# An H3 convolution and mixer kernel on one core: small loads as rows, angle arithmetic on ScalarE, and a re-dealt order of issue

## The chip, the core and the metric

The kernel runs on one core of a Trainium2 chip. A core has TensorE (PE, matrix products into PSUM), VectorE (DVE), ScalarE (ACT), GpSimd (POOL) and SyncE (SP, which here only starts DMA transfers). The metric is the device time of one execution in microseconds (us); lower is better.

## The reference

One sequence of S = 2048 tokens with D = 640 channels passes through two blocks, each with a conditioned LayerNorm in front and a gated residual behind:

```python
mod = (silu(c) @ w_mod).reshape(c.shape[0], 6, 1, -1)          # sa, ca, ga, sb, cb, gb
h = layernorm(x) * (1 + ca) + sa
x = x + ga * A_ref(h, k, v, shift_k, ssm_k, ssm_D)
h = layernorm(x) * (1 + cb) + sb
x = x + gb * B_ref(h, ...)

# A_ref
k_shift = sum(k_pad[:, t:t + S, :] * shift_k[:, ks - 1 - t] for t in range(4))
kv = k_shift * v
y = irfft(rfft(kv, 2 * S) * rfft(ssm_k, 2 * S))[:S] + kv * ssm_D
return q * y                                                     # q is the normed h

# B_ref
h = gelu(layernorm(x) @ w1)          # then four channel groups shifted by 1, -1, 2, -2 tokens
x1 = x + shifted(h) @ w2
return x1 + gelu(layernorm(x1) @ w3) @ w4
```

Here A_ssm_D and c are vectors of 640 values, and A_shift_k is a table of 640 x 4 values. D is folded into the long filter: it is added to the filter's first tap.

## The kernel before

Channels lie on the 128 partitions, in ND = 5 blocks of 128. The long convolution is a Fourier transform of length 4096 in two factors (64 x 64), done by matrix products. The stages are:

1. The filter A_ssm_k is loaded (tile Ra, five transfers at L228), D is added to its first tap (L444), each block is transposed on DVE into Rb (`to_slots`, L394), and `stage1` multiplies it with the small Fourier matrix F1bd (L407). Each result of 1024 columns is copied out of PSUM by ACT (L207) or DVE (L209) into T01.
2. `k_shift` (L463) applies the four-tap shift filter as products with diagonal matrices (tile RQ, built from skT by a POOL select at L355); DVE multiplies by v (L468). The products kv go through the same two stages.
3. `stage2_half` (L427) multiplies T01 with the second Fourier table Gs (in RG) into R3 for the filter and R5 for kv. Its groups go by k0, three of 32 at a time, in an order of their own.
4. `inverse1` multiplies both spectra on DVE (L617) and goes back by products with EA and EB (L628, L629); `inverse2` (L661) ends the transform.
5. `mod_half` (L493) makes the six modulation vectors from silu(c).
6. Then come the token tiles: LayerNorm chains (`chain_a`, `chain_b`, `chain_c`, `ln_finish`; L737 to L756, L702 to L717, sums of squares at L729), w1 (L818, L828), w2 (L873, L880), w3 (L907, L911), w4 (L928, L937), and the output.

The Fourier tables are computed in the kernel. `angles` makes integer angles: POOL counts (iota, L287), DVE multiplies and adds (L292), and masks (L293); ACT takes the sine (`sin_to`, L321). `angles_pool` does the same in floating point with a multiply-add (L306), a rounding (L308) and a subtraction (L310) on POOL or DVE; the sine is L316. F1bd is F1c put on a block diagonal by two POOL selects (L332, L333). Gs gets a first batch (kb = 0) by `angles` and a second (kb = 1) by `angles_pool`; a negated copy (L348) completes a batch. Then two transfers copy its upper half out (L353), and one copies the lower half into partitions 64 to 127 (L354), which must wait for the other two.

Every piece of work is a task with a number. The planner's `run` does not choose: the string ORDER lists all tasks in the order of issue, each with its engine (P, A, D, G for POOL, S for SP) and, for a task that takes PSUM, the places 0 to 3 of the four PSUM buffers. Each engine works through its tasks strictly in that order, and so does each DMA queue. Of the start, ORDER has on SP: D, blocks 1, 3, 2, 0 of A_ssm_k, the shift filter, block 4, and then the transposing loads of k and v (L233).

The three small operands are loaded with one element (or four) to a partition:

```python
dma("SP", 8, lambda q: ld_tiny(q, Dcol[:], A_ssm_D.rearrange("(b p) -> p b", p=P)), ...)
dma("SP", 8, lambda q: q.dma_start(skT[:], A_shift_k.rearrange("(b p) j -> p b j", p=P)), ...)
dma("SP", 8, lambda q: ld_tiny(q, c_col[:], c.rearrange("o (b p) -> p (o b)", p=P)), ...)
```

Of the kernel before, what the change touches and what calls it, by code (L numbers as in the profile page):

```python
# [8 lines left out]
BF = mybir.dt.bfloat16  # L9
F32 = mybir.dt.float32  # L10
I32 = mybir.dt.int32
ACT = mybir.ActivationFunctionType
# [14 lines left out]
0S 2S 19G 18D 50G 20D 21G 23D 22D 25A 4S 3S 1S 6S 27G 29D 36G 37G 28D 5S 8S 9S 11S 68G 10S 69D 24A 26G 88P:0 72G 73D 31A 30A 32D 38G 66D 89A 84P:1 85A  # L27
67D 90P:2 91A 86P:3 87D 39G 40A 102P:0 103A 100P:1 76P:2 70G 104P:0 41D 49G 101A 77A 42G 43G 105A 106P:3 107A 44A 45G 33S 47S 46S 71D 34S 12S 35S 48S
184S 181S 183S 182S 13S 14S 116P:1 92P:2 98P:0 74D 75D 117D 7S 99A 118P:3 119D 114P:0 15S 112P:1 113D 93A 110P:2 16S 115A 111A 96P:3 97A 94P:0 95D
82P:2 83A 80P:1 81A 78P:3 108P:0 51D 109A 52D 54A 56G 57D 53A 122P:2 79D 155P:1 156A 153P:0 154A 151P:3 152A 123D 157P:2 136D 120P:1 121D 173P:0 158A  # L30
55G 174A 171P:3 172A 177P:2 178D 175P:1 176A 161P:0 162D 141P:3 142A 167P:2 168D 147P:1 148A 58G 59G 163P:0 164D 165P:3 166A 137P:2 138A 145P:1 146A
230D 17S 149P:0 150A 190D 188D 126P:3 127D 139P:2 140A 60A 143P:1 199S 144A 124P:0 125D 179P:2 180A 187D 169P:3 170A 234P:1 235A 244P:2 159P:0 160A
128P:3 231D 242P:1 243A 245A 130P:0 61G 62G 186D 63G 64A 238P:1 239A 129D 131D 232D 248P:2 65G 196S 249A 246P:3 247A 185D 189G 191A 252P:0 202S 253A
134P:1 135D 132P:2 133D 236P:3 240P:1 237A 260P:0 261A 233D 250P:2 251A 241D 423D 200P:3 201A 258P:0 259D 319G 208S 192G 268P:2 269A 318S 197P:3 205S
198A 266P:1 267A 272P:2 273D 270P:3 271A 203P:0 284P:1 285A 292P:2 211S 204D 278P:3 279A 417D 276P:0 277A 342S 293D 426D 209P:1 210D 294P:2 295D 226S
290P:3 222G 291A 280P:1 281D 229G 227S 264P:0 274P:2 275D 343G 223G 265A 256P:3 262P:1 420D 206P:0 207D 257A 225G 254P:2 255D 282P:3 263A 286P:0
288P:1 287D 224G 312P:2 220S 283A 289A 212P:3 321D 320D 218G 213D 313A 328D 304P:0 305A 308P:1 316P:2 317A 217S 216G 302P:0 219S 214G 418D 228S 298P:2
215S 324P:3 325D 309A 221G 327G 326S 329D 322P:1 303A 336D 306P:0 299A 421D 323A 310P:2 296P:3 307A 334S 335G 337D 350S 297A 311A 300P:1 330P:0 301A
351G 332P:3 344D 345D 331A 314P:2 333A 315A 359G 340P:1 341A 338P:0 352D 348P:3 349A 353D 346P:2 358S 347A 360D 361D 354P:1 367G 339A 356P:3 368D 366S
369D 355A 364P:2 357A 375G 362P:0 376D 372P:1 374S 377D 401S 193A 363A 382S 370P:3 373A 384D 383G 385D 380P:0 378P:1 365A 392D 390S 391G 393D 422D  # L40
419D 424D 402P:2 427D 194D 403D 371A 388P:3 381A 379A 407S 389A 428D 386P:0 387A 416G 425D 396P:1 397A 394P:3 395A 398S 399P:0 400D 432P:12 429A 430D
434D 433A 489D 502A 510D 195G 413S 490D 491A 511D 530D 408P:3 513D 404S 405P:0 406A 531D 409A 512A 440S 492G 494D 475P:12 476A 477A 515D 532A 462P:03
463A 410S 411P:1 493G 495D 514G 435S 533D 534G 496A 497D 498G 441G 535D 464A 516D 536D 518D 499D 412A 517A 469P:20 537A 471A 519G 500P:3 538D 539G
414P:1 465G 470A 558D 449S 501D 520D 521P:3 436S 415A 507P:0 522A 443S 559D 560A 540D 541P:2 437S 542A 466P:13 431D 561D 562D 563A 564D 508A 546P:2
467D 468A 547A 548P:1 565G 448S 570D 528P:0 571D 566D 572D 567D 549A 573A 446S 568D 505P:3 506A 569A 574G 575G 447S 509G 529A 503D 523D 504D 621D 622D
472P:21 473A 526P:3 527A 623A 579D 580P:0 581A 576D 439S 543A 524D 577P:2 525D 624D 578D 625D 444S 438S 550P:3 627D 480S 551D 481S 626A 590P:0 591A
445S 482S 552A 588P:2 589A 595P:3 459D 628G 633D 629D 634D 553G 630D 631D 632A 635D 637D 636A 479S 554G 555D 556P:0 557A 592P:2 486S 596D 597A 638G
641A 639D 478S 488G 610P:3 612P:0 611A 593D 608P:2 606P:3 544D 594A 598D 613A 599G 474D 460A 603D 600D 601P:1 604P:0 609A 457D 607A 442S 454A 602A
640S 642S 651P:2 649P:3 461G 650A 450D 487S 652A 485S 605D 673P:0 667P:1 451D 545D 668A 674A 452G 582D 583D 484S 689D 690D 456A 458G 584D 585D 656P:3
692D 693D 653P:2 483S 614P:1 654D 655A 657D 694A 615D 659G 658A 671P:0 695D 660G 664D 665P:2 691A 661D 662P:3 663D 453D 669P:1 696G 701A 702D 703D  # L50
666A 735P:3 455G 672A 670A 697D 698D 699D 705G 737P:2 736A 739P:0 733P:1 616D 704A 643D 644D 645D 700A 738A 706G 709A 675P:32 710S 586D 587D 740A 755D
756D 757A 646A 707D 708S 758D 759D 717P:0 714D 761G 760A 762G 734A 763A 767D 777A 768D 711A 769D 719P:1 764D 780D 676P 718A 720A 721P:0 724P:1 647D
712D 765D 766A 677D 678D 770A 680S 771G 772G 683D 741P:32 648D 773D 774S 722D 775A 776S 785P:0 725D 726A 783P:1 713D 723A 824D 617S 825D 742P 821D
822D 827D 679S 681S 826A 743D 682S 727G 728G 731D 732S 823A 784A 828G 829A 786A 787P:3 729D 730S 833D 834D 835D 830D 831D 832A 837D 684D 685S 836A
620S 838G 790P:1 788D 789A 839D 840S 799P:0 791D 805P:3 806A 781D 841D 715D 716D 881D 749D 793G 792A 882D 842S 883A 803P:1 804A 794G 795A 796S 845P:2
846A 797D 778D 779D 884D 843P:3 844A 885D 887D 800A 801P:1 802A 618S 847P:2 848D 782D 941D 850P:3 851D 852A 886A 849A 619S 687S 798S 865P:0 866A
859P:1 860A 863P:2 807P:30 861P:1 744D 750D 753S 942D 944D 745S 853D 854G 855A 888G 893A 943A 752S 857A 889D 864A 945G 890D 856S 808P 858S 809D 891D
946A 947D 948D 950D 894D 862A 892A 895D 896A 897G 925P:2 926A 898G 751S 815D 747S 919P:3 901D 686S 920A 923P:1 899D 921P:0 949A 951G 922A 902S 900S
905P:2 906A 688S 903P:3 904A 952D 953S 956P:0 957A 954P:2 955A 907P:3 908D 910P:0 810D 958G 748S 959P:2 911D 913G 746S 816D 819S 924A 962P:1 867P:30
960D 817S 963D 813S 754S 912A 993P:2 909A 914G 812S 868P 915D 916S 917D 918S 977P:1 978A 994D 995A 996G 997G 971P:2 820S 972A 869D 998A 875D 927P:30  # L60
818S 964A 814S 811S 876D 961A 965D 966G 973P:1 967A 999S 969A 970S 870D 929D 974A 1028P:2 930D 975P:3 928P 968S 1000P:1 1001A 931S 935D 1002P:0 934S
976A 979P:13 981D 1003A 1006P:0 871S 873S 1004P:1 879S 1005A 872S 874S 936D 980P 987D 1029A 937S 933S 1026P:1 939S 1007A 877S 932S 988D 1024P:2 1025A
1032D 880S 878S 982D 983S 1008P:30 986S 991S 1027A 989S 1033D 1010D 938S 940S 1022P:2 1011D 1023A 1014S 1013S 1009P 1016D 984S 985S 1017D 1030P:13
1034D 992S 990S 1015S 1012S 1018S 1019S 1020S 1035D 1037S 1036S 1021S 1038S 1031P 1040D 1039S 1041D 1043A 1045A 1042S 1044S
# [72 lines left out]
def kernel(  # L137
# [51 lines left out]
    diagw = RQ[:, 0:2560].rearrange("p (b j m) -> p b j m", b=ND, j=4)  # L189
# [29 lines left out]
    c_col = mem.tile([P, ND], BF, name="c_col")  # L219
    skT = mem.tile([P, ND, 4], BF, name="skT")  # L220

    def ld_tiny(q, dst, src):
        with nc.allow_non_contiguous_dma(reason="tiny"):
            q.dma_start(dst, src)

    dma("SP", 8, lambda q: ld_tiny(q, Dcol[:], A_ssm_D.rearrange("(b p) -> p b", p=P)), w=[("Dcol", 0, 1)], rate=8.0)
    for b in range(ND):
        dma("SP", 512, lambda q, b=b: q.dma_start(sT[:, b, :], A_ssm_k[b * P:(b + 1) * P, :]), w=[("Ra", 2048 * b, 2048 * b + 2048)], rate=390.0)  # L228
    dma("SP", 8, lambda q: q.dma_start(skT[:], A_shift_k.rearrange("(b p) j -> p b j", p=P)), w=[("skT", 0, 1)], rate=30.0)
    dma("SP", 8, lambda q: ld_tiny(q, c_col[:], c.rearrange("o (b p) -> p (o b)", p=P)), w=[("ccol", 0, 1)], rate=12.0)  # L230
# [9 lines left out]
    b_neg = mem.tile([P, 1], F32, name="b_neg")  # L240
    stat = mem.tile([P, 3, 2, NT], F32, name="stat")
    s32 = mem.tile([P, 1], F32, name="s32")
    s32o = mem.tile([P, 1], F32, name="s32o")
    s64 = mem.tile([P, 1], F32, name="s64")
    s64t = mem.tile([P, 1], F32, name="s64t")
    pci = mem.tile([P, 2], I32, name="pci")
    offi = mem.tile([P, 2], F32, name="offi")
    offc = mem.tile([P, 6], F32, name="offc")

    def f(e):  # L250
        nc.vector.memset(mhalf[:], -0.5)
        nc.vector.memset(b_pos[:], PI_LO)
        nc.vector.memset(b_neg[:], -PI_LO)
        nc.vector.memset(stat[:], 0.0)
        nc.vector.memset(kT[:, :, 0:16], 0.0)
# [823 lines left out]
```

## Time and profile before

| | |
|---|---|
| Time, median of three runs (lowest, highest) | 301.91 us (301.49, 303.3) |
| Span of the profiled execution, first to last instruction | 298.7 us |
| Own time of the profiled execution beside its span | not given by the profile; 3.2 us lie between the span and the median |
| Busy: PE, DVE, ACT, POOL | 269.7, 218.2, 208.3, 104.8 us |
| Mean granted TensorE clock | 0.975 of full |
| DMA | 35.76 MB, 120 GB/s on average |
| Chain that ended last, by engine | PE 51%, DVE 13%, ACT 11%, DMA 10%, POOL 6%, issue 5% |

A profile comes from one execution on the chip. "L407" is line 407 of the kernel's file. A row names the engine, the operation, the tile written and the tile read with their shapes, a count, and a duration; "idle before <-X" is the time that the engine stood still just ahead, and what ended it. In the timeline the first column is the start in us from the span's start, the second the length. Neighbouring instructions of a kind are merged there ("x36"). A matmul's end is modelled, so a PE that is busy in every slice may still be paced by whoever empties its PSUM buffers.

### The profile page before, as it was taken

The page shows a single profiled execution, that of the slowest core. Times are in us where ns is not written, and L with a number is a line of the kernel's source. Part 1 is how long each engine was busy: PE and PEld are TensorE (multiplying, and loading weights), DVE is VectorE, ACT ScalarE, POOL GpSimd, SP SyncE. Part 2 cuts the span into 40 slices and gives each one's busy share as a digit, 9 for nine tenths or more (in the row PEclk, how much of TensorE's full clock was granted, in tenths as well). Part 3 has the DMA queues.
Part 4 walks back from the last instruction along what each step waited for, and adds up shares of the span by engine and source line. Part 5 has one row for each costly group of instructions (what it writes and reads, how often), then busy time and mean ns, then how long its engine had stood idle before and what let it go on. Part 6 is the DMA issues. An engine that isn't in the chain of part 4 may idle for free.

```text
span 298.7 us, 7890 instructions
## 1 busy us (share of the span) xinstructions
PE 269.7 (90%) x3176; PEld 208.5 (70%) x3182; DVE 218.2 (73%) x438; ACT 208.3 (70%) x341; POOL 104.8 (35%) x237
## 2 busy tenths in 40 slices
PE   0999999999989766869999999999999999999993
PEld 0666755777878436648878677787788767887871
DVE  8998999999999998898759589886361544212442
ACT  4799989999999789979868775766854705431200
POOL 5864364453216591434275426120421321100000
PEclk9999999999999859799999999999999999999999
DMA  6999999898999920563700203223113030510112
GB/s 215 275 215 184 225 137 246 225 217 221 229 253 281 280 65 2 153 203 69 273 4 0 46 5 68 56 46 60 41 40 80 5 89 6 63 43 23 29 52 60
DMA packets 58356, 35.76 MB, mean 120 GB/s; under 512 B 40032, under 2 KB 55008, under 8 KB 58320
## 3 DMA queue, kind: packets, MB, share of 16 engines
q1 hardware_dynamic: 57136, 32.01, 46.3%
q0 software_dynamic: 1088, 3.21, 4.1%
q8 instruction: 25, 0.41, 0.6%
q14 instruction: 11, 0.09, 0.1%
q10 hardware_dynamic: 96, 0.04, 0.1%
HBM read 16.31 MB, written 2.62 MB: 63 GB/s over the span
## 4 chain that ended last, share of the span: by engine, by line
PE 51%; DVE 13%; ACT 11%; DMA 10%; POOL 6%; issue 5%; SPq 2%; DVEq 0%; POOLq 0%; ACTq 0%
PE ps_w L937 17%; PE ps_w L907 14%; ACT T L207 5%; DMA Ra<-in_A_q_dram 5%; PE ps_w L873 4%; PE ps_w L818 3%; PE ps_s L427 3%; ACT RG L729 3%; DVE Rb L617 3%; PE ps_ksh L463 2%; POOL lnv L715 2%; PE ps_s L407 2%; DMA RK<-R 2%; DVE R L756 2%; PE ps_mod L493 2%
## 5 line engine op out<-in xcount | busy, mean ns | idle before, releaser
L907 PE MATMUL ps_w<-R,T 128*128 128x256 bf16 (+1 forms) x630 | 63.8, 261 | 0.7 <-DMA R<-RH 0.7
L907 PEld LDWEIGHTS <-T 128*128 128x128 bf16 x630 | 55.5, 98 | 7.9 <-issue 2.0
L937 PE MATMUL ps_w<-T,R 128*128 128x320 bf16 x416 | 59.1, 299 | 0.0
L911 ACT ACTIVATE R<-ps_w 128x1024 bf16<-128x1024 f32 (+2 forms) x36 | 28.8, 827 | 41.9 <-PE ps_w L907 41.9
L937 PEld LDWEIGHTS <-R 128*128 128x128 bf16 x416 | 40.5, 98 | 15.2
L960 DVE TENSOR_TENSOR T<-ps_w,R 128x640 bf16<-128x640 f32 x15 | 12.3, 822 | 35.4 <-PE ps_w L928 18.1
L207 ACT CAST T<-ps_s 128x1024 bf16<-128x1024 f32 x32 | 30.4, 1029 | 3.2 <-PE ps_s L407 3.1
L207 ACT CAST R<-ps_s 128x960 bf16<-128x960 f32 (+1 forms) x35 | 30.8, 964 | 1.8 <-PE ps_s L427 1.6
L407 PE MATMUL ps_s<-F1bd,Rb 128*128 128x256 bf16 x160 | 23.3, 298 | 8.7 <-DVE Rb L394 8.1
L729 ACT ACTIVATE RG<-R 128x640 bf16<-128x640 bf16 x32 | 23.5, 734 | 9.9 <-DVE R L880 6.7
L407 PEld LDWEIGHTS <-Rb 128*128 128x128 bf16 x160 | 16.7, 107 | 14.7 <-DVE Rb L394 8.6
L873 PE MATMUL ps_w<-RG,R 128*128 128x320 bf16 x160 | 23.2, 299 | 2.1 <-ACT R L820 2.1
L715 POOL TENSOR_TENSOR lnv<-lnv,mhalf 128x2 f32<-128x2 f32 (+1 forms) x29 | 22.5, 775 | 2.3
L427 PE MATMUL ps_s<-T,RG 64*128 64x160 bf16 x512 | 21.2, 230 | 0.8 <-ACT R L207 0.6
L880 DVE SCALAR_TENSOR_TENSOR R<-ps_w,R 128x640 bf16<-128x640 f32 x16 | 12.9, 819 | 11.8 <-PE ps_w L873 11.6
L427 PEld LDWEIGHTS <-RG 64*128 64x128 bf16 x512 | 17.7, 94 | 5.1 <-issue 4.6
L818 PE MATMUL ps_w<-R,RG 128*128 128x256 bf16 (+1 forms) x200 | 20.0, 259 | 1.3 <-DMA R<-RK 0.6
L873 PEld LDWEIGHTS <-R 128*128 128x128 bf16 x160 | 15.4, 98 | 8.2 <-ACT R L820 2.4
L629 PE MATMUL ps_i<-EB,Rb 128*128 128x128 bf16 x160 | 19.0, 219 | 1.5 <-DVE Rb L617 1.4
L818 PEld LDWEIGHTS <-RG 128*128 128x128 bf16 x200 | 17.1, 102 | 3.5 <-issue 2.0
L628 PE MATMUL ps_i<-EA,Rb 128*128 128x128 bf16 x160 | 19.0, 219 | 0.4 <-ACT R L207 0.3
L714 POOL TENSOR_TENSOR lnv<-stat,lnv 128x2 f32<-128x2 f32 x19 | 4.0, 212 | 40.9 <-ACT RG L729 28.7
(178 smaller groups left out, 513.5 us busy)
## 6 DMA issues: line engine op xcount, KB each, us to landing
Ra<-in_A_ssm_k_dram SPq DMA_DIRECT2D x5, 512.0 KB, 5.7
R<-in_w_mod_dram SPq DMA_DIRECT2D x6, 400.0 KB, 6.0
out_dram<-RH SPq DMA_DIRECT2D x60, 40.0 KB, 1.6
T<-in_B_w_dram SPq DMA_DIRECT2D x5, 432.0 KB, 6.2
RH<-in_w_mod_dram SPq DMA_DIRECT2D x4, 400.0 KB, 4.4
Ra<-in_A_q_dram SPq DMA_DIRECT2D x4, 320.0 KB, 6.6
RK<-R SPq DMA_DIRECT2D x5, 256.0 KB, 4.5
RK<-R POOLq DMA_DIRECT2D x5, 256.0 KB, 5.3
```

Source lines behind the costliest of these rows:

```text
L207: nc.scalar.copy(dst, src(ps.tile))
L407: nc.tensor.matmul(psv[:, ml, :], lhsT=xL[:, s0:s0 + P], rhs=F1r, start=True, stop=True)
L427: nc.tensor.matmul(psv[:, g, j], lhsT=Gs[p, k, 64 - 64 * cc:192 - 64 * cc], rhs=T1h[h][p, cc * 32 + k], start=(cc == 0), stop=(cc == 1), t ...
L628: nc.tensor.matmul(psv[:, w, :], lhsT=Av[:, r_, :, g_], rhs=EAf, start=True, stop=False)
L629: nc.tensor.matmul(psv[:, w, :], lhsT=Bv[:, r_, :, g_], rhs=EBf, start=False, stop=True)
L715: nc.gpsimd.tensor_tensor(rs, rs, mhalf[:, 0:n], ALU.pow)
L729: add("ACT", 0.74, lambda e: nc.scalar.activation(junk, src, ACT.Square, scale=float(D) ** -0.5, accum_out=stat[:, li, 1, t:t + 1]), r=[sk ...
L818: nc.tensor.matmul(pt[:, fb, 0:cw], lhsT=w1_sb[:, b, 160 * fb:160 * fb + P], rhs=hT[:, b, 0:cw], start=(b == 0), stop=(b == ND - 1))
L873: nc.tensor.matmul(pt[:, hf, 0:320], lhsT=gsf[:, fb, c0:c0 + P], rhs=w2_sb[:, fb, 320 * hf:320 * hf + 320], start=(fb == 0), stop=(fb == 4))
L907: nc.tensor.matmul(pt[:, fl, 0:cw], lhsT=w3_sb[:, b, fb * P:(fb + 1) * P], rhs=xT[:, b, 0:cw], start=(b == 0), stop=(b == ND - 1))
L911: nc.scalar.activation(g3[g % 2][:, f0:f0 + fn, 0:cw], ps.tile[:, 0:fn, 0:cw], ACT.Gelu_apprx_tanh)
L937: nc.tensor.matmul(bank(i, hf), lhsT=gg[:, fb, i * P:(i + 1) * P], rhs=w4_sb[:, fb, 320 * hf:320 * hf + 320], start=(fb == 0 and i == 0), ...
```

## The change

It has three parts.

**Rows.** D, c and the shift filter are loaded as five rows each (128, 128 and 512 elements) into a corner of T01 that is free at the start. TensorE turns them: a product with a 5 x 5 identity (`eye`, a POOL select) puts a row of 128 on 128 partitions. D takes one product and an ACT copy into Dcol; c and the four taps take five products and one ACT copy into `csk`, of which c_col and skT are now views. The diagonal matrices in RQ lie tap by tap instead of block by block.

**Angles.** The constant columns (`scol`) are split: nine operations stay on DVE, six go to a new POOL task (`scolt`). For the first batch of Gs, the multiply-add of `angles` leaves DVE for ACT (Identity with a scale and a bias column); DVE keeps the mask. The negated copy may now run on ACT too.

**Order.** The eight new tasks are put in, and some sixty tasks are moved in ORDER or given another engine. PSUM places change for 149 tasks.

```diff
@@ -216,18 +217,15 @@
-    dma("SP", 8, lambda q: ld_tiny(q, Dcol[:], A_ssm_D.rearrange("(b p) -> p b", p=P)), w=[("Dcol", 0, 1)], rate=8.0)
+    csk = mem.tile([P, 5 * ND], BF, name="csk")
+    c_col, skT = csk[:, 0:ND], csk[:, ND:5 * ND].rearrange("p (j b) -> p b j", j=4)
+    rowD, rowc, rows = T01[0:ND, 0:P], T01[0:ND, P:2 * P], T01[0:ND, 2 * P:6 * P]
+
+    dma("SP", 8, lambda q: q.dma_start(rowD, A_ssm_D.rearrange("(b p) -> b p", p=P)), w=[("T01", 0, P)])
...
-    dma("SP", 8, lambda q: q.dma_start(skT[:], A_shift_k.rearrange("(b p) j -> p b j", p=P)), w=[("skT", 0, 1)], rate=30.0)
-    dma("SP", 8, lambda q: ld_tiny(q, c_col[:], c.rearrange("o (b p) -> p (o b)", p=P)), w=[("ccol", 0, 1)], rate=12.0)
+    dma("SP", 8, lambda q: q.dma_start(rows, A_shift_k.rearrange("(b p) j -> b (p j)", p=P)), w=[("T01", 2 * P, 6 * P)])
+    dma("SP", 8, lambda q: q.dma_start(rowc, c.rearrange("o (b p) -> (o b) p", p=P)), w=[("T01", P, 2 * P)])
@@ -251,37 +250,62 @@
-    add("DVE", 1.9, f, r=[("pidx", 0, 1)], w=[("scol", 0, 1)])
+    add("DVE", 1.3, f, r=[("pidx", 0, 1)], w=[("scol", 0, 1)])
+
+    def f(e):
+        nc.gpsimd.tensor_scalar(s64t[:], s64[:], 1.0 / 8192, None, ALU.mult)
...
+    add("POOL", 1.0, f, r=[("scol", 0, 1)], w=[("scolt", 0, 1)])
+
+    add("POOL", 0.2, lambda e: nc.gpsimd.affine_select(out=eye, in_=one.to_broadcast([P, ND]), pattern=[[-1, ND]],
+                                                       compare_op=ALU.is_equal, fill=0.0, base=0, channel_multiplier=1),
+        r=[("consts", 0, 1), ("T01", 6 * P + 16, 6 * P + 17)], w=[("T01", 6 * P, 6 * P + ND)])
...
+        nc.tensor.matmul(pt[:, 0, 0:ND], lhsT=rowD, rhs=eye[0:ND, :], start=True, stop=True)
...
+    t1 = add("ACT", 0.2, lambda e: nc.scalar.copy(Dcol[:], psD.tile[:, 0, 0:ND]), w=[("Dcol", 0, 1)], use=psD)
...
+        nc.tensor.matmul(pt[:, 0, 0:ND], lhsT=rowc, rhs=eye[0:ND, :], start=True, stop=True)
+        for j in range(4):
+            nc.tensor.matmul(pt[:, 0, ND + ND * j:2 * ND + ND * j], lhsT=rows.rearrange("b (p j) -> b j p", j=4)[:, j, :], rhs=eye[0:ND, :], start=True, stop=True)
...
+    t1 = add("ACT", 0.2, lambda e: nc.scalar.copy(csk[:], psC.tile[:, 0, 0:5 * ND]), w=[("ccol", 0, 1), ("skT", 0, 1)], use=psC)
@@ -289,8 +313,12 @@
-                nc.vector.tensor_scalar(m_, ti, s_col, off, ALU.mult, ALU.add)
+                if not split:
+                    nc.vector.tensor_scalar(m_, ti, s_col, off, ALU.mult, ALU.add)
                 nc.vector.tensor_single_scalar(m_, m_, q - 1, ALU.bitwise_and)
+            if split:
+                add("ACT", 0.25 + 0.00095 * n, lambda e, m_=m_, off=off: nc.scalar.activation(m_, ti, ACT.Identity, scale=s_col, bias=off),
+                    r=[keys[0], ("scol", 0, 1)], w=[k_])
```

ORDER in the changed kernel, where it bears on what follows:

| Where | Before | After |
|---|---|---|
| SP, first issues | D, filter blocks 1, 3, 2, 0, shift filter, block 4; c much later (38.8 us) | block 3, D, block 1, shift filter, c, blocks 2, 0, 4 |
| ACT, first tasks | sines of F1c, sines of Gs | two multiply-adds of the angles, copy of Dcol, sines of F1c, sines of Gs, negation (first batch), copy of csk |
| PE, first tasks | stage 1 | product for Dcol, products for csk, stage 1 |
| Additions of D (L444) | blocks 1, 3, 2 POOL; 0, 4 DVE | blocks 3, 2, 4 POOL; 1, 0 DVE |
| Negation of Gs: first, second batch | DVE, POOL | ACT, DVE |
| Second batch, second angle: multiply-add, rounding, subtraction | DVE, POOL, POOL | POOL, DVE, DVE |
| H table, first multiply-add (L306 on RK) | DVE | POOL |
| Copies of Gs: three of batch 0, two of batch 1 | SP | POOL's queue |
| Stage-1 evictions, one each way | DVE and ACT | exchanged |
| LayerNorm statistics of two tiles (L539) | DVE | ACT |
| Norms: five, and two the other way | DVE, ACT | ACT, DVE |
| One transpose copy | ACT | DVE |
| First step of `ln_finish`, two groups | POOL | DVE |
| Two multiplies of q (L601) near 115 and 124 us, one w1 gelu | after the waits there | ahead of them; the gelu later |

Everything else keeps its engine, and nearly everything its neighbours. The output's transfers near the end are in a slightly different order.

## The prediction

> **What bounds the kernel now.** I read the page's rows by slice first, then windows of four microseconds, then the timeline of the first 26 us engine by engine, then the chain that ended last. The windows come first here (columns: window, length, busy us and instruction count of PE, weight loads, DVE, ACT, POOL, then clock, DMA share, GB/s).
>
> ```profile
> 8.00:10.00 2.00, 1.88 (x9) 1.35 (x10) 2.00 (x3) 0.81 (x1) 1.92 (x2) 1.00 1.02 328
> ...
> 20.00:24.00 4.00, 3.75 (x33) 2.98 (x32) 3.93 (x8) 4.00 (x6) 0.00 (x0) 1.00 0.89 189
> ...
> 116.00:120.00 4.00, 1.96 (x29) 1.64 (x27) 3.25 (x8) 3.90 (x10) 0.85 (x2) 0.98 0.00 0
> ...
> 128.00:132.00 4.00, 1.92 (x18) 1.45 (x17) 3.93 (x11) 3.69 (x9) 2.60 (x7) 1.00 0.86 287
> ...
> 180.00:200.00 20.00, 20.00 (x167) 15.86 (x166) 16.70 (x43) 12.37 (x27) 7.82 (x18) 1.00 0.30 63
> ```
>
> Three regimes follow. Until about 8 us nothing is multiplied. From 9 to 116 us DVE and ACT, which empty PSUM, are full, and PE follows them. From 116 to 140 PE is half idle while LayerNorm chains hop DVE, ACT, POOL. From 140 us PE has no gap worth speaking of, so the end is the moment it becomes full plus fixed work. A change counts only by how much earlier that moment comes.
>
> The start, in which most of the edit lies:
>
> ```profile
> 0.79 1.28 ACT L321 ACT_TABLE_LOAD   x1 [0.79 <-PEq L1063]
> ...
> 6.01 3.96 DVE L394 STREAM_TRANSPOSE Rb<-Ra 128x1024 int32<-128x1024 int32 x2
> ...
> 8.12 6.95 PE L407 MATMUL ps_s<-F1bd,Rb 128*128 128x256 bf16 x36 [8.12 <-DVE Rb L394]
> ...
> 9.19 2.84 ACT L207 CAST T<-ps_s 128x1024 bf16<-128x1024 f32 x3 [1.89 <-PE ps_s L407]
> ...
> 17.80 0.63 ACT L316 ACTIVATE RG<-R 128x512 bf16<-128x512 f32 x1 [0.52 <-POOL R L310]
> ```
>
> The first product waits for the first transpose, that for block 1 of A_ssm_k (landed 5.40) and its D add. Behind its table load ACT idles 2.06 us (to 4.13, for F1c's angles), 1.30 and 1.89 before its first eviction at 9.19; after that its only pause is 0.52 us at L316.
>
> The change, part by part.
>
> **Start.** (1) On DVE the scol step shrinks from 16 instructions (1.08 to 3.06) to 9; at the same spacing it ends near 2.4. Six go to POOL; its 128x1 rows are 189 to 354 ns, so 1.7 us, hidden, as POOL then waits for F1c. (2) ACT takes two 128x512 multiply-adds. The near row is L321 on 128x512, mean 715 ns, 1.34 us for two; on DVE they were 2 x 0.54. They stand first on ACT, and the built order of the changed kernel has a table load ahead of them, held until scol is done, and a second load ahead of the first Sin; before, one load ran at 0.79 for nothing. So: load 2.4 to 3.7, two Identity to 5.05, copy of Dcol to 5.35 (0.3, the 128x32 row), load to 6.65, two F1c sines to 7.2. Before, these ended at 4.66. (3) F1bd's two selects on POOL (2 x 0.42 and a gap) end at 8.15 instead of 6.84; the first product starts at 8.2 instead of 8.12. Slack eats nearly all 2.5 us. (4) ACT then has the RG sines (1.34), the negation (0.65, unseen on ACT; as its other 128x512 rows) and the copy of csk (0.25): free at 9.4, where 9.19 stood. (5) The add for block 3 stands behind F1bd on POOL, 8.35; DVE wants it at 7.95 and loses 0.4.
>
> Here two rules of the Trainium skill bear, both in "ScalarE: Activation LUTs". "What ACT_TABLE_LOAD costs" puts a switch at 2.66 us with its drain; the row of this kernel's other load, L834, is 1.28 (115.56 to 116.84, next ACTIVATE at 116.85), so I add 1.28; by the rule the first product would start 1.4 to 2.8 us later. "Rules for kernel authors" gives multiplies and adds to VectorE. Rows agree per piece (0.54 against 0.7), but ACT was idle here, so I book the load, not the pieces. That the load is needless (the page's "Table sets: the hidden batching unit" has identity in every set, and L547's Identity at 50.27 runs on the Sin set with no load between) changes nothing: the built order has it.
>
> **Rows and loads.** Dcol's load of single elements landed in 3.0 us, skT's in 6.6, c_col's in 5.0. As rows of 256 and 1024 bytes they are not in the trace: at least the 1.5 us of a 20 KB store, at most as before. SP now issues block 3 first, then D, block 1, rows, c. By bytes moved (770 KB by 5.40, some 400 KB/us after 4) a second half megabyte ahead costs block 1 about 0.7 us and the vanished element packets give about that back: 5.4 to 5.6, and at worst, with nothing given back, 5.40 + 0.51/0.4 = 6.7. D lands between 4 and 5, under the Identities. Six little products (a 98 ns weight load each) and two copies lie in idle PE and counted ACT time. The products of csk wait for c and the filter rows in front of the first stage-1 product, so rows landing after 8.2 would hold PE; expected 5.9. SP spends one more issue (0.58) ahead of the transposes, and none later.
>
> **POOL and DVE to 26 us.** POOL, 1.3 late, does L308 (1.97), a DMA issue (0.5), L310 (1.28), one add, the diagonal select (2.46): RQ ready near 15.0, not 13.07; PE wants it at 14.91, so 0.2 late. The second L308 and L310 and a negation leave POOL (4.7 us) for DVE (about 0.4 + 0.55 + 0.74; the TENSOR_SCALAR rows on DVE are 0.43 to 0.57), DVE gives away two L306 (1.1), one negation (0.74); evictions swap evenly. DVE's sum is level, 0.5 late by the lost add and the wait for POOL's L306. ACT's 0.52 pause goes. The last stage-1 eviction is DVE's: stage 2 starts at 26.05 instead of 25.79. Book **+0.3**; ends -0.3 (the pause alone counts) and +1.5 (block 1 late).
>
> **The RG copies (L353, L354).** Five of six go from SP to POOL's queue. They cost POOL 0.5 to 0.8 each (its L613 issues). The second-batch lower copy waits there for two landings, and the first-batch lower copy and E's eight products stand behind it: issue 26.3, landing 30 to 31 (POOL copies landed in 4.0 to 6.0). Stage 2 needs it at its ninth group, about 31.7. Book 0; uncovered, up to 1.5. SP, freed, starts later transposes about 2 us earlier, but DVE and PE, not they, set the pace there: 0.
>
> **76 to 116 us.** DVE is full with the same work: 0.
>
> **112 to 140 us.** The chain as it runs now (start, us, engine, tile, line); a LayerNorm factor leaves POOL, the DVE norms follow at once, statistics sit between them and the next wait, and PE gets its transposes at the end:
>
> ```profile
> 123.84 0.21 POOL lnv L717
> 124.07 0.80 DVE RK L594 x2
> ...
> 128.86 0.81 DVE ln_st L539 x2
> ...
> 140.31 0.73 PE ps_tr L772 x10
> ```
>
> A multiply L601 (0.40, at 120.30 on the chain) moves into the 0.68 wait before 116.96 (-0.4), one into the 1.15 wait before 124.07. One RK norm (0.4) and one ln1 statistics (1.1) go to ACT, a transpose copy (0.4) and an RQ norm (0.4) come back. ACT gains 0.92 + 1.86 and loses 0.69 + 0.94: +1.15 in a stretch where it idles about 2. A gelu of w1 is deferred, which lets the squares before 122.76 end 0.5 earlier. Followed through: DVE's norms at 128.65 instead of 129.87, but ACT's statistics put the L820 gelu 0.6 later, and PE's L873 at 131.8 with it; the w3 evictions then free PSUM only 0.3 earlier. Of 1.1 us on DVE, **-0.3** reaches PE; ends -1.2 and +0.6.
>
> **After 140.** The second statistics move leaves 1.1 us of DVE and fills ACT's 2.32 wait before 156.47; norms follow. PE idles only 0.6 in 160:180 and 0.65 in 200:220: **-0.4**, between -1.2 and +0.5. The tail's outputs are reordered only: 0.
>
> Sum: +0.3 - 0.3 - 0.4 = -0.4 on a span of 298.7. The page gives no other time for the profiled execution; 3.2 us lie between its span and the median of 301.91, and I keep them: **301.5**. A measurement of this kernel tells about 1% (3 us) from no change.
>
> **Rivals.**
> A. The balance pays more: LayerNorm gains reach PE whole (-1.2 - 1.2), the start loses nothing (-0.3): -2.7, 299.2; with PE's clock not falling to 0.5 between 120 and 123 (3 us at half rate, 1.5) 297.7. For: 6 us of PE gaps between 116 and 136. Against: ACT is 3.7 of 4 busy there.
> B. Slower, by one mechanism: ACT is in order, and the Dcol copy, which waits for D's row behind 512 KB, stands before the F1c sines. If D lands later than 5.0, each microsecond delays load, sines, F1bd, all products. At 7.5, beyond skT's 6.6 us after issue at 1.3, it is +2.5, with the +0.3: 304.3; with switches by the skill's 2.66 it passes 305. For: block 1's 4.08 us landing. Against: D alone took 3.0.
> C. The lower RG copy lands after 31.7: +1.5, 303.0.
> D. The ACT load does not do what it says: nothing of DVE's relief reaches the chain and all ends cancel, 301.9; that is in the forecast's own range.
>
> **Chances.** Forecast 0.60 (own range 300.3 to 302.9), A 0.18, B 0.12, C 0.10. Faster by over 1% needs 298.9, the far half of A and some unseen: 0.12. Slower by over 1% is B's far end: 0.10. Same 0.78. Eight in ten: 298.9 to 303.9.
>
> **What would show it.** Two ACT_TABLE_LOAD rows before 7 us; first L439 product between 8.1 and 8.6; first eviction on ACT at 9.4; no POOL pause before the second L344; stage 2 (L459) from 26; PE full from about 140. Wrong if the first product starts after 9.5, if L459 waits for a DMA of RG near 31, or if PE is full before 138.

## The result, and the profile after

The changed kernel takes 305.88 us (median of six runs, 305.03 to 307.63) against 301.7 us for the kernel before (six runs, 300.42 to 303.71). The ratio is **1.0139**, 95% interval [1.0105, 1.0172]: slower by 1.4%, where 301.5 us and no measurable change had been forecast. The span of the profiled execution went from 298.7 to 303.3 us. Its own time is 305.18, so 1.9 us lie around the span; other executions of the kernel before have 1.7 us there. The 298.7 shown ahead therefore belongs to one of its quickest executions, near 300.4, and the 3.2 us that the forecast added were partly the distance of that execution from the median.

Lines of changed code have new numbers: stage 1 is L439 (was L407), the block transposes L426 (L394), the add of D L476 (L444), stage 2 L459 (L427), RQ's select L387 (L355), the angle steps on POOL L334, L336, L338 (L306, L308, L310), ACT's evictions L208 (L207), the copies of RG L385 and L386 (L353, L354). Here is the start in the timeline of the changed kernel (start, length, engine, line, operation):

```profile
2.24 1.28 ACT L320 ACT_TABLE_LOAD   x1 [2.24 <-DVE offc L271]
...
5.12 1.28 ACT L349 ACT_TABLE_LOAD   x1
...
7.34 0.16 DVE L476 TENSOR_TENSOR Ra<-Ra,Dcol 128x1 bf16<-128x1 bf16 x1 [1.62 <-DMA Ra<-in_A_ssm_k_dram]
7.54 3.96 DVE L426 STREAM_TRANSPOSE Rb<-Ra 128x1024 int32<-128x1024 int32 x2
...
9.65 5.30 PE L439 MATMUL ps_s<-F1bd,Rb 128*128 128x256 bf16 x24 [3.61 <-DVE Rb L426]
...
10.82 1.28 POOL L338 TENSOR_TENSOR R<-R 128x512 f32<-128x512 f32 x1
...
11.39 3.29 DVE L476 TENSOR_TENSOR Ra<-Ra,Dcol 128x1 bf16<-128x1 bf16 x1
...
12.06 0.19 POOL L476 TENSOR_TENSOR Ra<-Ra,Dcol 128x1 bf16<-128x1 bf16 x1
12.20 2.46 POOL L387 TENSOR_SCALAR_AFFINE_SELECT RQ<-csk 128x2560 bf16<-128x2560 bf16 x1
...
14.72 2.06 DVE L426 STREAM_TRANSPOSE Rb<-Ra 128x1024 int32<-128x1024 int32 x1
...
16.83 0.39 PE L439 MATMUL ps_s<-F1bd,Rb 128*128 128x256 bf16 x2 [1.88 <-DVE Rb L426]
```

Read it from the bottom. PE starves for 1.88 us at 16.83 because the transpose of filter block 0 began at 14.72. DVE began it late because of the row at 11.39: an add of **one column** of 128 numbers that took **3.29 us**. The same add for block 1, further up, took 0.16. Its row shows no wait: a wait for a semaphore would stand in brackets as idle time. POOL's rows beside it are the lead: the add runs while POOL works through L338, its own L476 and the select, and ends at 14.68 where the select ends at 14.66. The upper rows hold a second, smaller loss: block 1 of the filter was waited for until 7.34, so the first product came at 9.65 instead of 8.12.

In the kernel before, the same stretch looks like this; the add for block 0 (L444) starts 0.08 us ahead of the select and takes 0.15 us:

```profile
9.18 1.28 POOL L310 TENSOR_TENSOR R<-R 128x512 f32<-128x512 f32 x1
...
9.87 0.74 DVE L348 TENSOR_SCALAR RG<-RG 128x512 bf16<-128x512 bf16 x1
...
10.53 0.15 DVE L444 TENSOR_TENSOR Ra<-Ra,Dcol 128x1 bf16<-128x1 bf16 x1
10.61 2.46 POOL L355 TENSOR_SCALAR_AFFINE_SELECT RQ<-skT 128x2560 bf16<-128x2560 bf16 x1
```

The same windows as ahead of the prediction, with the stretch from 16 us added (window, length, then busy us and count of PE, weight loads, DVE, ACT, POOL, then clock, DMA share, GB/s):

```profile
8.00:10.00 2.00, 0.34 (x2) 0.28 (x3) 2.00 (x2) 0.76 (x3) 2.00 (x3) 1.00 1.37 354
16.00:20.00 4.00, 2.70 (x15) 1.70 (x16) 4.00 (x4) 3.23 (x4) 1.95 (x3) 0.81 1.10 212
20.00:24.00 4.00, 4.00 (x20) 2.04 (x19) 3.90 (x5) 1.21 (x2) 0.00 (x0) 0.77 0.31 68
116.00:120.00 4.00, 2.06 (x18) 1.46 (x16) 3.42 (x9) 3.48 (x8) 2.06 (x14) 0.50 0.00 0
128.00:132.00 4.00, 2.92 (x94) 2.40 (x90) 3.04 (x7) 3.94 (x10) 3.07 (x9) 1.00 0.54 173
180.00:200.00 20.00, 19.93 (x157) 14.77 (x155) 15.25 (x39) 14.40 (x30) 7.12 (x17) 1.00 0.23 48
```

In 20 to 24 us ACT is busy 1.21 us (before: 4.00) and PE does 20 products at 0.77 of its clock (before: 33 at full clock). Where PE, DVE and ACT were all full, ACT now stands idle most of the time, and only DVE does as much as before. Stage 2 starts late by the whole sum of this (the kernel before, then the changed one):

```profile
25.79 1.83 PE L427 MATMUL ps_s<-T,RG 64*128 64x160 bf16 x44 [0.16 <-ACT T L207]
```

```profile
31.25 1.83 PE L459 MATMUL ps_s<-T,RG 64*128 64x160 bf16 x44
```

That is 31.25 against 25.79, 5.5 us. Later landmarks keep the offset, as the chain that ended last shows: RK's norm at 141.39 against 135.48 (5.9), the transposes at 146.04 against 140.31 (5.7). Again the kernel before comes first:

```profile
135.48 0.63 DVE RK L594
```

```profile
140.12 0.20 POOL lnv L746
...
141.39 0.63 DVE RK L626
...
146.04 0.56 PE ps_tr L804 x10
```

By the end it is 4.6. So in these two executions everything was lost before 31 us, and about 1 us came back after 150.

### The profile page after: what moved, and what is told of

Same layout as the page of the kernel before. It is cut to its first block, busy times and chain, and to the rows that moved or that the text cites. A ratio compares the mean times of both kernels' runs of the same rounds, so it can differ in the third digit from the quotient of the medians.

```text
span 303.3 us, 7927 instructions
## 1 busy us (share of the span) xinstructions
PE 272.6 (90%) x3188; PEld 209.6 (69%) x3188; DVE 217.4 (72%) x428; ACT 216.8 (71%) x357; POOL 106.8 (35%) x246
## 4 chain that ended last, share of the span: by engine, by line
PE 60%; DVE 17%; ACT 13%; issue 4%; DMA 3%; POOL 0%; SPq 0%; DVEq 0%; ACTq 0%; POOLq 0%
PE ps_w L969 16%; PE ps_w L939 16%; PE ps_w L905 6%; ACT T L208 4%; PE ps_s L459 4%; PE ps_ksh L495 4%; PE ps_w L850 4%; DVE Rb L649 4%; PE ps_s L439 3%; ACT R L208 2%; ACT RG L761 2%; DMA Ra<-in_A_ssm_k_dram 2%; PE ps_mod L525 2%; DVE Ra L772 1%; DMA R<-RK 1%
## 5 line engine op out<-in xcount | busy, mean ns | idle before, releaser
L208 ACT CAST T<-ps_s 128x1024 bf16<-128x1024 f32 x32 | 30.7, 1027 | 7.6 <-PE ps_s L439 7.5
L208 ACT CAST R<-ps_s 128x960 bf16<-128x960 f32 (+1 forms) x35 | 31.0, 975 | 2.6 <-PE ps_s L459 2.3
L439 PE MATMUL ps_s<-F1bd,Rb 128*128 128x256 bf16 x160 | 23.8, 297 | 6.4 <-DVE Rb L426 5.5
L439 PEld LDWEIGHTS <-Rb 128*128 128x128 bf16 x160 | 16.4, 105 | 13.0 <-DVE Rb L426 6.6
L459 PE MATMUL ps_s<-T,RG 64*128 64x160 bf16 x512 | 21.3, 230 | 1.1 <-ACT R L208 1.0
L459 PEld LDWEIGHTS <-RG 64*128 64x128 bf16 x512 | 17.8, 94 | 5.6 <-issue 4.8
L495 PE MATMUL ps_ksh<-R,RQ 128*128 128x512 bf16 x80 | 20.2, 400 | 0.1
```

Source lines behind the costliest of these rows:

```text
L208: nc.scalar.copy(dst, src(ps.tile))
L439: nc.tensor.matmul(psv[:, ml, :], lhsT=xL[:, s0:s0 + P], rhs=F1r, start=True, stop=True)
L459: nc.tensor.matmul(psv[:, g, j], lhsT=Gs[p, k, 64 - 64 * cc:192 - 64 * cc], rhs=T1h[h][p, cc * 32 + k], start=(cc == 0), stop=(cc == 1), t ...
L495: nc.tensor.matmul(pt[:, i, :], lhsT=diagw[:, b, jj, :], rhs=kT[:, b, c0:c0 + 512], start=(jj == 0), stop=(jj == 3))
```

## The experiments

Ratios are against the kernel before, run beside each kernel on the same chip. "The add" below is DVE's L476 (L444 in forms of the kernel before) for block 0. A change of lines like `2S ... 4S` is one in ORDER.

**1. Block 1 ahead of block 3 (e1).**

```diff
-4S 18D 19G 27G 20D 33G 0S 22G 58G 2S 44G ...
+2S 18D 19G 27G 20D 33G 0S 22G 58G 4S 44G ...
```

> The changed kernel with the loads of filter blocks 1 and 3 exchanged in SP's order, nothing else: block 1 goes out at 0.8 us and block 3 behind D's row. Theory L (two costs add up: block 1 landed 1.5 us late because block 3 was issued ahead of it; DVE's add for block 0 stood 3.3 us): block 1's add at about 5.8, first stage-1 product about 8.1 instead of 9.65, the add for block 0 still stands until the select on POOL ends, stage 2 starts 0 to 1.5 us earlier than 31.3, span 301.8 to 303.3. Rival C (the copies of RG that went to POOL set the start of stage 2): first product earlier all the same, stage 2 unmoved at 31.3, span 303.3.

Measured: 301.14 us, ratio **0.9971** [0.9953, 0.9989]. One exchange of two loads takes back all of the loss, not 1.5 us of it. The timeline shows why:

```profile
7.99 5.28 PE L439 MATMUL ps_s<-F1bd,Rb 128*128 128x256 bf16 x24 [1.91 <-POOL F1bd L361]
...
10.06 0.13 DVE L476 TENSOR_TENSOR Ra<-Ra,Dcol 128x1 bf16<-128x1 bf16 x1
10.81 1.30 POOL L338 TENSOR_TENSOR R<-R 128x512 f32<-128x512 f32 x1
```

DVE now comes to the add at 10.06, 0.75 us ahead of POOL's L338, and it takes 0.13 us. The two losses were not a sum: the late load pushed DVE into POOL's busy stretch. Stage 2 starts at 26.12.

**2. The adds with one SBUF tensor (e2), and both edits (e3).**

```diff
-    Dcol = mem.tile([P, ND], BF, name="Dcol")
+    Dcol = mem.tile([P, ND], F32, name="Dcol")
-    eng_of[e].tensor_tensor(sT[:, b, 0:1], sT[:, b, 0:1], Dcol[:, b:b + 1], ALU.add)
+    eng_of[e].tensor_scalar(sT[:, b, 0:1], sT[:, b, 0:1], Dcol[:, b:b + 1], None, ALU.add)
```

> The changed kernel with Dcol kept in f32 and the five adds of D written as tensor_scalar with Dcol's column as its scalar, so that DVE's add for block 0 reads one tensor from SBUF instead of two; engine and place in the order are the same. Theory L with the shared port (an add with two SBUF inputs on DVE waits while POOL works on SBUF): L476 at 11.4 takes 0.15 to 0.3 us instead of 3.29, block 0's transpose starts at about 11.7, stage 2 starts 2.5 to 3.5 us earlier, near 28, span about 300.5. Rival M (the add waited for something that its form doesn't change, such as block 0's landing or D's column): it still ends at 14.7, span 303.3. Rival C (RG's copies on POOL): the add is short and stage 2 stays at 31.3, span 303.3.

> Both edits together: filter block 1 loaded ahead of block 3, and the adds of D as tensor_scalar with one SBUF tensor. Theory L: the first 31 us lose nothing of the 5.5 but what the clock takes, stage 2 starts at 26 to 27, and what the changed order gains after 160 us stays: span 297.7 to 299, ratio to the kernel before 0.996 to 1.0. Rival C (RG's copies on POOL set stage 2): stage 2 starts no earlier than 29, span 301 or more.

Measured: 302.17 us, 1.0006 [0.9985, 1.0027] for e2, and 301.9 us, 0.9995 [0.997, 1.0021] for e3. The stall is gone in both (0.22 and 0.20 us), and stage 2 starts at 26.97 and 26.41. So the late load by itself costs 0.6 us of stage 2 rather than 1.5. As a proof of the mechanism e2 is weak: there block 1 was in at 6.64, and the add at 10.74 came just ahead of L338 at 10.93, so it might have passed in its old form too. (Experiment 6 later shows an add of the old form at almost this place, and it was held.)

**3. The stall made in the kernel before (e4).** One POOL task goes forward; nothing else differs from the kernel before.

```diff
- ... 70G 104P:0 41D 49G ...
+ ... 49G 70G 104P:0 41D ...        # 49: RQ's select, 70: add of D, block 2
```

> The kernel before with one move in POOL's order: RQ's select (L355) ahead of the add of D for block 2 (L444) that it followed, so that it is running when DVE comes to the add for block 0 at 10.5 us. If the port explains the stall: DVE's L444 takes about 2.4 us instead of 0.15 and ends with the select near 12.9; block 0's transpose starts 2.3 us later; the start of stage 2 moves from 25.8 to 27 or 28 and the span from 298.7 to 300 or 301. If the stall belonged to the changed kernel's own waits, L444 stays at 0.15 us and the span at 298.7.

Measured: 304.14 us, **1.0082** [1.0049, 1.0115], which is 2.5 us. Its timeline:

```profile
10.47 2.52 POOL L355 TENSOR_SCALAR_AFFINE_SELECT RQ<-skT 128x2560 bf16<-128x2560 bf16 x1
10.59 2.42 DVE L444 TENSOR_TENSOR Ra<-Ra,Dcol 128x1 bf16<-128x1 bf16 x1
...
13.04 2.04 DVE L394 STREAM_TRANSPOSE Rb<-Ra 128x1024 int32<-128x1024 int32 x1
```

The add takes 2.42 us instead of 0.15 and ends with the select. In the kernel before it had started at 10.53 and the select at 10.61. Those 0.08 us had kept that kernel quick. The margin is small but steady: the three kernels of experiment 9 share this start, and their traces have 0.07 to 0.08. In each, DVE's negation L348 just ahead of the add ends 0.14 to 0.15 us after POOL's L310, and the select begins where L348 ends, so DVE and POOL stay in step.

**4. The number of inputs (e5, e5b).** POOL is kept at work without the gap that L385's issue makes between L336 and L338, in both forms of the add, with the changed kernel's own order of loads.

```diff
- ... 46G 42G ... 47G ... 78G 57G ...
+ ... 46G ... 47G ... 78G 57G 42G ...     # 42: issue of a copy of RG
```

> The changed kernel with its own order of loads, the one-input adds, and one move on POOL: the issue of RG's copy that stood between L336 and L338 goes behind the select, so that POOL works on SBUF without a gap from 8.1 to about 13.8 us and DVE's add for block 0 (10.7 to 11.4) falls inside it whatever the load's landing. If the port is what stalls and the number of SBUF inputs decides: L476 on DVE takes 0.2 to 0.3 us in the middle of L338 or of the select. If any add of this kind is stalled by POOL: it takes 2 to 3 us and ends with the select, near 13.9.

> The control to the kernel with the one-input adds and POOL busy without a gap: the same move of RG's copy behind the select, the adds as they are in the changed kernel, with two SBUF inputs. If the number of inputs decides: L476 on DVE is stalled, 2 to 3.5 us long, and ends with the select at about 13.9. If the move itself changed something else: L476 takes 0.2 us here too.

Measured (one run each): e5 302.68 us, e5b 303.57 us. The one-input add fell in the middle of L338 and was not held:

```profile
10.22 1.28 POOL L338 TENSOR_TENSOR R<-R 128x512 f32<-128x512 f32 x1
...
10.91 0.17 DVE L476 TENSOR_SCALAR Ra<-Ra,Dcol 128x1 bf16<-128x1 bf16 x1
```

The control failed: in e5b the add came at 11.30, just as L338 ended (10.12 + 1.28), and took 0.15 us ahead of the select. Its add tells nothing about two inputs. A later pair of rows in e5b does. L338 is here on DVE, a subtraction of two SBUF tensors, beside POOL's L334:

```profile
17.22 0.81 POOL L334 TENSOR_SCALAR RK<-RK,s32o,offc 128x512 f32<-128x512 int32 x1
17.50 1.07 DVE L338 TENSOR_TENSOR R<-R 128x512 f32<-128x512 f32 x1
```

It took 1.07 us and ended 0.54 after L334. In e6 (experiment 8) it met L334 too, and again took 1.07 and ended 0.54 after it. In the other nine traces with this row it took 0.69.

**5. The changed kernel once more.** No edit.

> The changed kernel as it is, once more, beside the kernels of this call. Two things are asked: where block 1 lands in another execution (7.3 us in the first, but 6.6 and 6.8 in two kernels with the same order of loads), and whether DVE's add for block 0 is stalled then too. POOL's L338 begins at 10.8. If block 1 lands before about 6.8, the add gets in ahead of L338, takes 0.15 us, and the time is near 302; if it lands later, the add stands until the select ends, 3 us and more, and the time is near 306. Ratio 1.010 to 1.017 if the stall is the rule.

Measured: 306.94 us, 1.0138 [1.0112, 1.0165]. Block 1 was in by 6.47, and my expectation was wrong: the add came ahead of L338 and stood still longer than ever.

```profile
9.97 0.80 POOL L385 DMA_DIRECT2D RG<-RG  x1
10.47 4.96 DVE L476 TENSOR_TENSOR Ra<-Ra,Dcol 128x1 bf16<-128x1 bf16 x1
10.81 1.27 POOL L338 TENSOR_TENSOR R<-R 128x512 f32<-128x512 f32 x1
...
14.66 0.75 POOL L334 TENSOR_SCALAR R<-R,s64t,offc 128x512 f32<-128x512 int32 x1
```

At 10.47 POOL was issuing the copy of RG that the change had put on it. The add got through neither between L385 and L338 nor between the select and L334; it ended at 15.43 with L334. In e1 the add at 10.06, 0.08 us after the same issue had begun, did pass. Whether the issue itself holds the add, or only leaves no gap ahead of L338, was not separated.

**6. The sine's table set first (e8), then with one-input adds (e9).** e8 is e1 with a 128x1 sine on ACT ahead of everything.

```diff
-        nc.vector.memset(b_neg[:], -PI_LO)
+        nc.vector.memset(b_neg[:], -PI_LO); nc.scalar.activation(pre[:], b_neg[:], ACT.Sin)
```

> The changed kernel with block 1 loaded first and one 128x1 sine on ACT behind the memset of its input, ahead of everything else there, so that ACT loads the table set of the sine at about 1 us and Identity and sines share it. If it works: one ACT_TABLE_LOAD instead of two, F1c's sines end 1.3 us or more earlier, F1bd is ready by 6.7 instead of 7.9, the first product then waits for Rb alone (7.9, 0.1 us earlier), and stage 2 starts 0.1 to 0.4 us earlier than 26.1; ratio 0.995 to 0.997. If the second load stays: no change, 0.997.

Measured: 305.12 us, 1.0082 [1.0052, 1.0111]. One table load remains at the start, at 0.79, and the first product starts at 6.82, 1.2 us earlier than in e1. The kernel is slower all the same:

```profile
8.89 0.80 POOL L385 DMA_DIRECT2D RG<-RG  x1
...
9.57 4.07 DVE L476 TENSOR_TENSOR Ra<-Ra,Dcol 128x1 bf16<-128x1 bf16 x1 [0.46 <-DMA Ra<-in_A_ssm_k_dram]
9.73 1.27 POOL L338 TENSOR_TENSOR R<-R 128x512 f32<-128x512 f32 x1
```

Everything moved forward, POOL by more than DVE, which had to wait for block 0; so the add met POOL again, and stage 2 started at 30.63. This was the control that e5b had failed to be. e9 changes nothing in it but the adds' form (the diff of e2).

> The kernel with block 1 first and the sine's table set first, which was slower because its add for block 0 stood 4.07 us (9.57 to 13.64, beside POOL's copy issue, L338 and select), with one edit more: the adds of D as tensor_scalar with one SBUF tensor. If the number of SBUF inputs decides: the add at about 9.6 takes 0.2 us beside the same work on POOL, and since stage 2 began 16 us after the end of that add in every form of the changed kernel so far, it begins at 25.6 to 26.2 instead of 30.6; ratio 0.992 to 0.998. If something else held that add (block 0's landing, the sine's order): it still ends near 13.6, ratio 1.008.

Measured: 300.59 us, **0.9945** [0.9922, 0.9968]. The add takes 0.22 us, and stage 2 starts at 25.92:

```profile
9.25 0.81 POOL L385 DMA_DIRECT2D RG<-RG  x1
...
9.95 0.22 DVE L476 TENSOR_SCALAR Ra<-Ra,Dcol 128x1 bf16<-128x1 bf16 x1 [0.47 <-DMA Ra<-in_A_ssm_k_dram]
10.09 1.30 POOL L338 TENSOR_TENSOR R<-R 128x512 f32<-128x512 f32 x1
```

Beside POOL the two adds stand at the same place: 0.68 us after the issue began and 0.16 ahead of L338 in e8, 0.70 and 0.14 in e9. With e4 and e5 this settles the mechanism as far as these runs go: the add with two SBUF tensors is held by POOL's work, the same add written with one is not. What in the form decides is not separated, because the edit changes the instruction, Dcol's type and the number of tensors at once. For the number speaks that DVE's transposes (L426), which read one tensor, kept 2.0 us each beside POOL's L336 and the issue in the changed kernel (7.54 to 11.50). e9 is the best version found, with e10 beside it, and faster than both kernels.

**7. Block 0 sooner (e10).** e9 with the loads of blocks 0 and 2 exchanged (`1S` and `3S`).

> The same, with the loads of filter blocks 0 and 2 exchanged, because DVE waited 0.46 us for block 0 before its add at 9.57. If the end of block 0's add sets the start of stage 2: the add ends near 9.3 to 9.4 and stage 2 begins 0.3 to 0.4 us earlier than in the kernel without the exchange; ratio 0.991 to 0.997. If the landing of block 2, then needed later, or the two last blocks set it: stage 2 where it was or later by up to 0.5 us.

Measured: 300.66 us, 0.9949 [0.9923, 0.9974], the same as e9. The add ended 0.25 us sooner (9.92), stage 2 began no sooner (26.01). This expectation missed: without a stall the add did not set the pace here. The trace is not a clean test, for PE waited for c's row until 7.82, and the first product came at 8.06 instead of e9's 7.03.

**8. RG's copies back on SP (e6).** e3 with tasks 41, 42, 43, 54, 56 as S instead of G.

> The changed kernel with block 1 loaded first and the one-input adds, and in addition RG's five copies given back to SP at their places in the order. If POOL as issuer costs nothing: stage 2 starts at 26.1 to 26.7 as it did with both edits, ratio to before within 0.002 of 0.9995. If the lower copies on POOL set the start of stage 2 (rival C of the prediction): stage 2 at 25.5 to 25.9 and 0.5 us gained. If SP is held up by the copies' waits: the transposing loads of k and v come later, k_shift waits for them, and 0.5 to 1.5 us are lost.

Measured: 301.34 us, 0.9984 [0.9968, 1.0]; stage 2 at 26.70. The intervals of e3 and e6 overlap: with the stall gone, the queue of these copies costs or brings nothing that shows.

**9. The rest of the change alone.** The kernel before with its own order up to a place where both orders have issued the same set of tasks, and from there the order and engines of the changed kernel: from about 150 us, from about 45 us, and from 150 us with seven moves between engines undone.

```diff
- the ORDER of before, 1046 tasks
+ its first 650, then that of the changed kernel             # late only
+ its first 213, then that of the changed kernel             # from 45 us
+ late only, with 461A 705A 739A 849A on D, 709D on A, 713D 769D on G   # numbers of the changed kernel
```

> The kernel before with its own order up to the stage where the mixer's tokens turn to w3 and w4 (about 150 us), and from there the order and engines of the changed kernel (the last norms and squares, without anything of the start or of the middle). Theory G (the offset between the two traces fell from 5.7 us near 155 us to 4.6 at the end, so the late order is worth about 1.1 us): span 297.6 against 298.7, ratio 0.995 to 0.998. Rival N (that 1.1 us is the clock or a peculiarity of the one trace of before): ratio 0.999 to 1.001.

> The kernel before with its own order up to about 45 us, and from there the order and engines of the changed kernel, so all of the change but its start. Theory G: the late gain of 1.1 us and in the middle (45 to 150 us) next to nothing, since the offset between the two traces stays between 5.6 and 6.2 us there: ratio 0.994 to 0.998. If the middle loses what it seems to lose around 100 us: 0.5 us worse than the kernel with the late order alone. Rival N: 0.999 to 1.002.

> The kernel before with the late order of the changed kernel, but with the seven late single moves between engines undone (one tile's statistics, three norms and three small steps around them back on DVE, ACT or POOL as before): only the sequence is new. If the engines make the late gain (norms from DVE to ACT): ratio 0.999 to 1.001. If the sequence makes it: 0.996 to 0.998, as with the engines moved.

Measured: 0.9971 [0.9957, 0.9985] for the late part, 0.9972 [0.9954, 0.999] from 45 us, and 0.9996 [0.9973, 1.002] with the engines put back. The late order brings about 0.9 us (1.0 by the medians, 300.81 against 301.83), the middle nothing that these intervals of 0.5 us each way can show. Of the two halves of the late part, the engine moves look like the source, as the third kernel loses the gain; but its interval overlaps that of the first, so this is not shown. The windows from 156 us, one execution each, point the same way (late only, then engines back):

```profile
156.00:180.00 24.00, 24.00 (x209) 19.46 (x208) 19.39 (x50) 19.67 (x35) 9.07 (x23) 1.00 0.08 16
```

```profile
156.00:180.00 24.00, 23.18 (x201) 18.51 (x199) 18.28 (x46) 18.10 (x30) 9.20 (x26) 1.00 0.08 16
```

ACT has 1.6 us more to do in this stretch, and PE, which stood idle for 0.82 us, is full.

One table holds the start together (us, from each timeline; the last column is the distance from the end of the add to stage 2):

| kernel | add starts | takes | ends | stage 2 | distance |
|---|---|---|---|---|---|
| before | 10.53 | 0.15 | 10.68 | 25.79 | 15.1 |
| e4, select first | 10.59 | 2.42 | 13.01 | 28.04 | 15.0 |
| changed | 11.39 | 3.29 | 14.68 | 31.25 | 16.6 |
| changed, again | 10.47 | 4.96 | 15.43 | 31.43 | 16.0 |
| e1, block 1 first | 10.06 | 0.13 | 10.19 | 26.12 | 15.9 |
| e2, one input | 10.74 | 0.22 | 10.96 | 26.97 | 16.0 |
| e8, sine first | 9.57 | 4.07 | 13.64 | 30.63 | 17.0 |
| e9, sine first, one input | 9.95 | 0.22 | 10.17 | 25.92 | 15.8 |

Stage 2 follows the end of the add at 15 us in the old order, and at 15.8 to 17.0 in the new one. By this count the changed kernel's 5.5 us are 4.0 of a later add and 1.5 of distance. Of the distance, 0.8 goes with the new order (e1's 15.9 against 15.1). The other 0.7 is not explained: PE's clock was lower behind the stall (eight products of L495 from 19.09 took 3.27 us, the next eight 1.89), but the second execution, with the longer stall, has only 0.1 of it.

## Why the prediction was wrong, point by point

- **Start, steps (1) to (5): right in kind, mostly in size.** Two table loads came before 7 us, each 1.28 us, as the row said, and not the 2.66 that the Trainium skill gives for a switch with its drain ("ScalarE: Activation LUTs", "What ACT_TABLE_LOAD costs"). F1c's sines ended at 6.95 (7.2 predicted), Dcol's copy took 0.14 us instead of 0.3. In the changed kernel itself the first product came at 9.65, past the 9.5 that the prediction had named as a sign of being wrong, and ACT's first eviction at 11.58 instead of 9.4, both through the late block 1. e1, where block 1 is on time, starts its first product at 7.99 (8.2) and stage 2 at 26.12 (26.05): the +0.3 of the start is about what the change costs when nothing collides.
- **Rows and loads: the landing was off.** Block 1 was expected at 5.4 to 5.6, at worst 6.7. In five executions with this order of loads DVE waited for it until 6.47 to 7.34 (5.40 was its landing before). The estimate let the vanished element packets give back what block 3 in front takes; the sum did not come out so. With block 1 issued first (e8), DVE had it by 4.49.
- **POOL and DVE to 26 us: the step that failed.** It summed DVE's work from the durations of single rows, found the sum level, and booked +0.3. The add for block 0 stood in that sum at its 0.15 us. It took 3.29, because the change had delayed POOL's L338 and select (select at 12.20 instead of 10.61) and DVE's add (11.39 instead of 10.53) by different amounts, and the margin of 0.08 us was gone. The prediction followed POOL's delay closely (RQ ready near 15.0; measured 14.66) but asked only who waits for RQ, not what else runs on DVE meanwhile. The end "+1.5 (block 1 late)" had the trigger and about a quarter of the price.
- **A sign that stood in the trace of before.** The prediction took DVE's negation at the 0.74 us of its row L348. That row was very likely lengthened by POOL itself, though no run tested it. It ran beside POOL's L310 and took 0.74 to 0.87 in five traces with this start (the kernel before, e4 and experiment 9), ending 0.14 to 0.15 after L310 each time. The same operation on DVE in the eleven traces of the new order (L380) took 0.27 to 0.32. If so, a row's duration already held a wait for another engine, and the sum carried it on as work.
- **A rule that I had not weighed.** The Trainium skill says in "SBUF — State Buffer", section "Who interferes with whom", that a DVE instruction with two SBUF inputs contends with a GpSimd instruction that reads SBUF, and that one with a single input outside the fast modes does not. e4, e5, e8 and e9 agree (2.42, 0.17, 4.07, 0.22 us). The page's "Summary: rules for kernel authors" adds that the second to issue blocks until the first finishes. Here it was worse: the add missed the gaps between three and four POOL instructions in a row.
- **The needless second load.** "Changes nothing: the built order has it" was right for this kernel; one early sine removes it (e8, e9), so Identity did run on the sine's set.
- **RG copies, 0: right.** e6 moves nothing that shows. Rival C's wait did not come either: L459 has no wait for a DMA, although the lower copies were issued only at 29.0 and landed 5.8 to 6.7 us later; stage 2 was late by as much.
- **112 to 140, -0.3: not found.** Ratio 0.9972 with the middle, 0.9971 without; 0.3 us would lie within these intervals. **After 140, -0.4: right in sign, booked at half its size.** 0.9 us, within its own end of -1.2.
- **Rivals.** B had the slower side with 304.3, but by D's row; D's row was on PE at 4.25 and Dcol copied at 5.10, so it never came near. (Its 304.3 also counts the start's 0.3 twice, which 301.5 already holds.) No rival had two engines stopping each other. Together they left 0.10 for slower by over 1%. Had block 1 been loaded first, the 301.5 would have been met (301.14), partly by luck: the middle brought nothing, the late part twice what was booked, and the collision would have gone unseen.

## What to carry to other kernels

A sum of row durations holds only while the engines don't touch. For each short DVE instruction that reads two SBUF tensors, look at what POOL runs in the same microseconds, before and after the change, and treat a margin of a tenth of a microsecond as none. When one row is ten times longer than its twins and no wait stands in its brackets, look for the instruction of another engine that ends when it ends. The remedy here was a form of the 128x1 add with a single SBUF tensor, which took 0.16 to 0.22 us wherever it fell in these runs. For larger instructions one tensor seems to be no guarantee, as L348 and the rows below suggest.

## What the runs showed of the hardware that was not expected

- A 128x1 add of two bf16 tensors on DVE took 0.13 to 0.19 us where POOL did not hold it and 2.42, 3.29, 4.07 and 4.96 us beside POOL's work (and once 0.27, in e5b for block 1, ending with POOL's L360). It was not always let in where one POOL instruction followed another: at 12.06 to 12.20 in the changed kernel it had two such places and used neither, in e5b it slipped in at one.
- The load of 512 KB issued first was there by 4.49 us; the one issued 0.87 us later was waited for until 6.47 to 7.34, in executions of the same order of loads.
- Larger instructions with one SBUF tensor took longer beside POOL too (read from the traces, not tested by a run). DVE's L336 (128x512 f32) took 0.88 in e5b and 0.57 in e6 beside POOL's count (L330), ending 0.29 us after it both times, and 0.37 to 0.45 in nine other traces. It also went the other way: POOL's add L476 took 0.55 in e3 and e10 beside DVE's L336, ending 0.05 to 0.06 us after it, and 0.27 to 0.31 elsewhere in this form.
- PE's granted clock was 0.61 and 0.53 in 18 to 20 and 20 to 22 us of the changed kernel, soon after PE's wait of 1.88 us for the stalled DVE, and 0.50 from 16 to 20 us in e8 after a wait of 4.10. It stayed at full from 16 to 24 us in e1 and e9, and also in e4, where PE had waited 1.75 us. What decides was not tested.
